# Transposing P per token tile, and gating as if no row were routed, with two rows replaced in DRAM

## The chip, the core and the metric

One core of a Trainium2 chip. The metric is device time in microseconds of one execution, the median of the runs; the profile is of one execution. The engines are called by the profile's names: PE is TensorE, DVE VectorE, ACT ScalarE, POOL GpSimd, SP the engine that issues most DMAs; SPq and ACTq are the issuing queues of SP and ACT.

## What is computed

Token matrix x of 2048 x 640, in bfloat16. It is normalized row by row; an attention over the last 512 keys of each of 32 heads (head size 192) and a small routed MLP both start from it, and the second gates the first:

```python
xn = _layernorm(x, axis=-1)
s = _A_ref(xn, A_k_cache, A_v_cache, A_wq, A_wo)      # softmax(q k') v, then wo
g = _silu(_B_ref(xn, B_w_r, B_w_gate, B_w_up, B_w_down))
return x + s * g
```

In `_B_ref`, r = xn @ w_r picks the C = 2 rows with the largest scores; only these two go through the MLP, and their result is added to their rows of xn:

```python
g = _silu(x_sel @ w_gate)
u = x_sel @ w_up
y = (g * u) @ w_down
r_sel = _sigmoid(jnp.take_along_axis(r, idx, axis=1))
y = y * r_sel.reshape(B, C, 1)
return x + upd.reshape(B, S, D)     # upd: zero but for the two rows of y
```

So for 2046 of the 2048 rows the gate is silu(xn) alone.

## The kernel before

**The loop.** Heads go in 8 groups of 4 (two pairs each); tokens in 4 tiles of 512. A step is (group, token tile, pair), 64 steps, each of two blocks: block b (0 to 127) handles 256 tokens as two tiles of 128 (a = 0, 1) against one pair of heads. Blocks 0 to 11 and 126 to 127 are written out by hand (`FIRST`, `LAST`); blocks 12 to 125 follow one list, `BLOCK`, whose tokens are emitted in this order:

- A, B: the two halves of q's products for the next step (L340); after B, ACT copies q out of PSUM (L352). The pool for q has one pair of banks, so the next A waits for that copy.
- S0, S1: scores of the two token tiles (L367), two PSUM buffers; M0, M1: their row maxima on DVE (L372); E0, E1: exponentials on ACT (L377) into `p_ring`, which holds two blocks.
- P: `o_item(b - 2)`: P times V (L406) for both token tiles, division by the row sum (reciprocal L413; scaled copies L417 on DVE, L420 on ACT), and the transpose of the result, oT, by a DMA that SP issues (L423). Between the two tiles' products `bg[b]` is emitted.
- W: `w_item(b - 6)`: the products with wo (L447), added to the fp32 accumulator `s_acc` on DVE (L470).
- m: what stands in `mid[b]`; l, the end of the block: `end[b]`, then `loads[b]`.

Every engine executes its own instructions in the order in which they were emitted, SP and the other DMA queues too. The row sums come for free: V has a further column of ones (L175), so that the products of P with V carry the sum in column 192.

**P's transpose.** `exps` issues a DMA transpose of P on SP: for blocks in `SPLIT` one per token tile, 128 x 1024, right behind that tile's exponentials (L381); for the others one of both tiles, 128 x 2048, behind E1 (L383). `pT_ring` holds three blocks. P's exponentials of block b may not overwrite `p_ring` before block b - 2 has been read by its transpose.

**The routed rows.** In dictionaries by block (`bg`, `mid`, `end`, `loads`) the kernel plans the MLP beside the loop. `m_r` (blocks 12 to 27) makes the scores; `m_round`, `m_rows`, `m_top`, `m_sel`, `m_tok`, `m_own` find the two rows (the scores are turned by a TensorE transpose, L690) and fetch their x by an indirect DMA on POOL; `m_gather` normalizes the two rows on DVE (blocks 34 to 40, L774 at the end); `m_xsT` turns them; `m_ffn` makes gate and up products (L787) at blocks 42, 49 and 57, with h on DVE (L797, L798), turned by SP (L801); `m_down` the down products (L826) at 62 and 69, and `m_sum` (block 70) adds four partial sums on POOL (L839 to L842). Then y is written to DRAM and read back to all 128 partitions (L844, L846). Weights of the MLP are loaded by ACT's queue in blocks 33 to 66.

**The gate.** For each of 16 tiles n of 128 tokens, `m_add(n)` at block 71 + 2n halves xn on POOL (L850) and adds each of the two rows of y, times a column that is 0.5 in the routed row and 0 elsewhere (L853, L854): five POOL operations of 128 x 640. `m_gate(n)` takes tanh on ACT at block 75 + 2n (L860) and multiplies on DVE in the middle of block 76 + 2n (L863), in place in xn. From block 107 on, `fin_load` fetches x again (L912), `fin_pre` multiplies `s_acc` by the gate and adds x on POOL (L917, L918), and in the last head group `w_item` multiplies the last products by the gate (L473), adds (L475, L478) and stores.

Of the kernel before, what the change touches and what calls it, by code (L numbers as in the profile page):

```python
# [21 lines left out]
def kernel(ctx, tc, A_x, A_k_cache, A_v_cache, A_wq, A_wo, B_x, B_w_r, B_w_gate, B_w_up, B_w_down, out):  # L22
    nc = tc.nc
    P = 128
# [147 lines left out]
    eps_t = const.tile([P, 1], FP32, name="eps_t")  # L172
    nc.vector.memset(eps_t, EPS)
    nc.vector.tensor_copy(out=ident, in_=ident_f)
    nc.gpsimd.memset(v_ring[:, :, :, Dh:Dh + 1], 1.0)  # L175

    mv = const.tile([P, NTB, 2], FP32, name="mv")
    rstd = const.tile([P, NTB], FP32, name="rstd")
# [108 lines left out]
    NS = len(steps)  # L287
    NB = 2 * NS
    HEAD = 12
    SPLIT = (0, 1, 2, 3, NB - 4, NB - 3, NB - 2)  # L290
    qT_of = {}
    fin_x = {}
    fin_pool = {}
# [355 lines left out]
    def m_open():  # L649
        late.close()  # L650
        M["stack"] = ExitStack()
        M["w"] = M["stack"].enter_context(tc.tile_pool(name="moe_w", bufs=1))
        M["s"] = M["stack"].enter_context(tc.tile_pool(name="moe_s", bufs=1))
        M["wr"] = M["s"].tile([P, D], BF16, name="wr_bc", tag="t3")
        nc.gpsimd.dma_start(out=M["wr"], in_=B_w_r.partition_broadcast(P))
        M["r"] = M["s"].tile([P, NTB], FP32, name="r_pn")
        M["xsT"] = M["s"].tile([P, DC, 32], BF16, name="xsT")
        M["xsel"] = M["s"].tile([32, D], BF16, name="xsel")
        nc.gpsimd.memset(M["xsel"], 0.0)
        M["pick"] = M["s"].tile([P, 2], FP32, name="pick")  # L660
        nc.gpsimd.memset(M["pick"], 0.0)
        for c in range(4):
            nc.gpsimd.affine_select(out=M["pick"], in_=M["pick"], compare_op=ALU.not_equal, fill=1.0, base=-32 * c,
                                    pattern=[[-1, 2]], channel_multiplier=1)
        M["oh"] = M["s"].tile([P, NTB, 2], FP32, name="oh")
        M["iota"] = M["s"].tile([P, NTB], FP32, name="iota")
        nc.gpsimd.iota(M["iota"], pattern=[[P, NTB]], base=0, channel_multiplier=1, allow_small_or_imprecise_dtypes=True)

    def m_r(n):
        def f():  # L670
# [6 lines left out]

    def m_round():

        M["r_b"] = M["s"].tile([P, NTB], BF16, name="r_b")  # L680
        nc.vector.tensor_copy(out=M["r_b"], in_=M["r"])
        M["base"] = M["s"].tile([NTB, 1], FP32, name="base")
        nc.gpsimd.iota(M["base"], pattern=[[0, 1]], base=0, channel_multiplier=P, allow_small_or_imprecise_dtypes=True)
        M["cpos"] = M["s"].tile([P, NCD], FP32, name="cpos")
        nc.gpsimd.iota(M["cpos"], pattern=[[1, NCD]], base=0, channel_multiplier=0, allow_small_or_imprecise_dtypes=True)

    def m_rows():

        r_ps = f_tile([NTB, P], BF16, "r_ps")
        nc.tensor.transpose(out=r_ps, in_=M["r_b"], identity=ident)  # L690
        M["rows"] = M["s"].tile([NTB, P], FP32, name="r_rows", tag="t2")
        nc.vector.tensor_copy(out=M["rows"], in_=r_ps)

    def m_top():

        top = M["s"].tile([NTB, 8], FP32, name="top8")
        loc = M["s"].tile([NTB, 8], U32, name="loc8")
        nc.vector.max(out=top, in_=M["rows"])
# [33 lines left out]
    def m_own():  # L732
        sel = M["s"].tile([2, 2, 2], FP32, name="sel")
        for q in range(2):
            nc.vector.tensor_tensor(out=sel[:, q, :], in0=M["best"][0:2, q, :], in1=ident_f[0:2, 0:2], op=ALU.mult)
        M["own"] = M["s"].tile([2, 2], FP32, name="own")
        nc.vector.reduce_sum(out=M["own"], in_=sel, axis=AX.X)
        idx_i = M["s"].tile([2, 1], I32, name="idx_i")
# [14 lines left out]

    def m_gather():

        def mask():
            for j in range(2):
                nc.vector.tensor_scalar(out=M["oh"][:, :, j], in0=M["iota"], scalar1=M["best"][:, 1, j:j + 1], scalar2=0.5,
                                        op0=ALU.is_equal, op1=ALU.mult)

        def begin():
            M["mv2"] = M["s"].tile([2, 2], FP32, name="mv2")
            M["rs2"] = M["s"].tile([2, 2], FP32, name="rs2")
            ln_stats(M["xg"], M["mv2"], parts=2)
            M["nw"] = rsqrt_newton(M["mv2"][:, 1:2], M["rs2"][:, 0:1], 2, 1)

        def newton(q):
            for f in M["nw"][3 * q:3 * q + 3]:
                f()

        def apply():
            mv2, rs2 = M["mv2"], M["rs2"]
            ln_nmr(mv2[:, 0:1], rs2[:, 0:1], rs2[:, 1:2])
            nc.vector.tensor_scalar(out=M["xsel"][0:2, :], in0=M["xg"], scalar1=rs2[:, 0:1], scalar2=rs2[:, 1:2], op0=ALU.mult, op1=ALU.add)  # L774
        return [mask, begin] + [lambda q=q: newton(q) for q in range(4)] + [apply]

    def m_xsT():
        nc.sync.dma_start_transpose(out=M["xsT"], in_=M["xsel"])
# [2 lines left out]
    def m_ffn(fb):  # L781
# [12 lines left out]
        def act():  # L794
            th = M["th"]
            M["h"] = M["s"].tile([P, P], BF16, name="h")
            nc.vector.scalar_tensor_tensor(out=th[:, 2], in0=th[:, 2], scalar=1.0, in1=th[:, 0], op0=ALU.add, op1=ALU.mult)  # L797
            nc.vector.scalar_tensor_tensor(out=M["h"], in0=th[:, 2], scalar=0.5, in1=th[:, 1], op0=ALU.mult, op1=ALU.mult)  # L798

        def turn():  # L800
            nc.sync.dma_start_transpose(out=M["hT"][:, fb * 4:(fb + 1) * 4, :].rearrange("p c t -> p (c t)"), in_=M["h"])  # L801
# [10 lines left out]
    def m_sig():  # L812

        sg = M["s"].tile([P, 2], FP32, name="sg")
        nc.scalar.activation(out=sg, in_=M["best"][:, 0, :], func=ACT.Tanh, scale=0.5)
        nc.vector.tensor_scalar(out=sg, in0=sg, scalar1=0.5, scalar2=0.5, op0=ALU.mult, op1=ALU.add)
# [18 lines left out]
    def m_sum():  # L835
# [4 lines left out]
        y_sb = M["s"].tile([2, D], BF16, name="y_sb", tag="t3")  # L840
        nc.gpsimd.tensor_tensor(out=y4[:, 0:2, :], in0=y4[:, 0:2, :], in1=y4[:, 2:4, :], op=ALU.add)
        nc.gpsimd.tensor_tensor(out=y_sb, in0=y4[:, 0, :], in1=y4[:, 1, :], op=ALU.add)  # L842
        y_d = tc.dram_tile([2, D], BF16, name="y_d")
        nc.gpsimd.dma_start(out=y_d, in_=y_sb)  # L844
        M["y_bc"] = M["w"].tile([P, 2, D], BF16, name="y_bc", tag="w")
        nc.gpsimd.dma_start(out=M["y_bc"], in_=y_d.partition_broadcast(P))  # L846

    def m_add(n):
        def f():
            nc.gpsimd.tensor_scalar(out=xn[:, n, :], in0=xn[:, n, :], scalar1=0.5, scalar2=None, op0=ALU.mult)  # L850
            for j in range(2):
                yh = M["s"].tile([P, D], BF16, name="yh", tag="t1")
                nc.gpsimd.tensor_scalar(out=yh, in0=M["y_bc"][:, j, :], scalar1=M["oh"][:, n, j:j + 1], scalar2=None, op0=ALU.mult)  # L853
                nc.gpsimd.tensor_tensor(out=xn[:, n, :], in0=xn[:, n, :], in1=yh, op=ALU.add)  # L854
        return f

    def m_gate(n):
        def a():
            M["tz"] = M["s"].tile([P, D], FP32, name="tz", tag="t2")
            nc.scalar.activation(out=M["tz"], in_=xn[:, n, :], func=ACT.Tanh)  # L860

        def b():
            nc.vector.scalar_tensor_tensor(out=xn[:, n, :], in0=M["tz"], scalar=1.0, in1=xn[:, n, :], op0=ALU.add, op1=ALU.mult)  # L863
        return a, b

    bg[11].append(m_open)

# [3 lines left out]
        spot(b).append(m_r(n))  # L871
    end[24].append(m_r(15))
    mid[28].append(m_round)
    bg[28].append(m_rows)
    for b, it in enumerate((m_top, None, m_sel, m_tok, m_own, *m_gather())):
        if it is not None:
            spot(29 + b).append(it)
    loads[40].append(m_xsT)
# [15 lines left out]
    bg[69].append(m_down(1))  # L894
    bg[70].append(m_sum)
    for n in range(NTB):
        bg[71 + 2 * n].append(m_add(n))
        a, b = m_gate(n)
        bg[75 + 2 * n].append(a)
        mid[76 + 2 * n].append(b)  # L900


    def fin_open():
# [5 lines left out]
    def fin_load(n):  # L909
        def f():  # L910
            fin_x[n] = fin_pool["x"].tile([P, D], BF16, name="x_fin")
            nc.sync.dma_start(out=fin_x[n], in_=x_v[:, n, :])  # L912
        return f

    def fin_pre(n):
# [101 lines left out]
```

## Time and profile before

| | |
|---|---|
| runs, device time | 795.93 us median of 3 (792.62, 795.93, 797.04) |
| profiled execution, device time | 794.4 us |
| its span | 792.6 us |
| PE clock granted | 1.00 |
| SP: oT transposes (L423) | 126, 1209/1235/2445 ns (min/median/max) to issue |
| SP: x again (L912) | 16, 399/799/1311 ns to issue, 160 KB each, 3.5 us to landing |
| DMA queue 1 (SP's) | 130.83 MB, 433568 packets, 94.6% of 16 engines' span |
| HBM | read 39.98 MB, written 2.62 MB |

How to read the profile: a line such as L372 is a line of the kernel. A group's row gives out<-in, count, busy us, mean ns of one, and the idle time of the engine before them with what ended it. In a timeline row the first number is the start in us, the second the length, x the number of merged instructions, and the bracket the idle time before the first with what released it. For a DMA the row of SPq is the issue alone; landing is later. In the view of one tile, three numbers after the count are shortest, median and longest in ns. In the waits, the three numbers are us in total, times, and the longest.

### The profile page before, as it was taken

To read this page: it belongs to the slowest core of one execution; us is meant where nothing else is said; L and a number is where in the kernel's file an instruction comes from. 1 tells how busy PE (TensorE), PEld (TensorE's weight loads), DVE (VectorE), ACT (ScalarE), POOL (GpSimd) and SP (SyncE) were. 2 spreads that over 40 slices of the span, in tenths; PEclk is the share of its full clock that TensorE was granted. 3 is DMA by queue.
4 is the path that set the end of the run, shared out by engine and by line. 5 is a ranking of instruction groups with operands and counts; after the bars stand their busy time and mean duration, and the time that the engine had idled before them with its cause. 6 is when DMAs were issued, how large, how long until landed. Compare 5 with 4: busy or idle time off the path is not lost.

```text
span 792.6 us, 26635 instructions
## 1 busy us (share of the span) xinstructions
PE 778.2 (98%) x11357; PEld 576.8 (73%) x11357; DVE 594.5 (75%) x1091; ACT 526.1 (66%) x952; POOL 313.8 (40%) x248
## 2 busy tenths in 40 slices
PE   8899999999999999999999999999999999999997
PEld 4457677777777776777777777777777777777775
DVE  7898788877777676767666777777777776766785
ACT  6676666666666766666666667767777776666662
POOL 1334111021110101001001499998996413565865
PEclk9999999999999999999999999999999999999999
DMA  9989999799999999999999999989999899999993
GB/s 233 196 175 168 164 188 165 149 191 164 180 205 173 184 221 195 183 178 216 182 206 167 180 190 183 155 158 184 158 191 164 148 190 179 197 185 168 180 173 87
DMA packets 443319, 141.77 MB, mean 179 GB/s; under 512 B 410436, under 2 KB 442696, under 8 KB 443200
## 3 DMA queue, kind: packets, MB, share of 16 engines
q1 hardware_dynamic: 433568, 130.83, 94.6%
q10 hardware_dynamic: 8672, 6.72, 3.4%
q0 software_dynamic: 960, 2.52, 1.1%
q8 instruction: 89, 1.46, 0.8%
q14 instruction: 30, 0.25, 0.1%
HBM read 39.98 MB, written 2.62 MB: 54 GB/s over the span
## 4 chain that ended last, share of the span: by engine, by line
PE 89%; DMA 4%; DVE 3%; ACT 2%; issue 1%; SPq 0%; ACTq 0%; DVEq 0%
PE w L447 25%; PE q_ps L340 23%; PE o_ps L406 20%; PE s L367 19%; DMA pT<-pexp 4%; ACT pexp L377 1%; PE q_ps L309 1%; DVE nm L372 1%; DMA v_sb<-in_A_v_cache_dram 1%; ACT xnT L283 0%; DMA x_in<-in_A_x_dram 0%; PE tp L282 0%; PE gu_ps L787 0%; DVE fin_t L473 0%; DVE fin_o L475 0%
## 5 line engine op out<-in xcount | busy, mean ns | idle before, releaser
L372 DVE TENSOR_REDUCE nm<-s 128x2 f32<-128x1024 f32 x256 | 313.0, 1223 | 123.1 <-PE s L367 117.2
L377 ACT ACTIVATE pexp<-s,nm 128x512 bf16<-128x512 f32 x512 | 324.3, 689 | 110.5 <-DVE nm L372 67.7
L340 PE MATMUL q_ps<-xnT,wq_g 64*128 64x512 bf16 (+1 forms) x2340 | 232.8, 323 | 1.1 <-ACT qT L352 1.0
L447 PE MATMUL w<-wo_g,oT 64*128 64x320 bf16 x3072 | 231.1, 296 | 0.4 <-ACT o_sb L420 0.2
L367 PE MATMUL s<-kT,qT 64*128 64x512 bf16 x1536 | 211.8, 376 | 1.7 <-ACT pexp L377 1.4
L447 PEld LDWEIGHTS <-oT 64*128 64x128 bf16 x3072 | 171.5, 94 | 57.2 <-issue 1.2
L406 PEld LDWEIGHTS <-pT 64*128 64x128 bf16 x4096 | 177.6, 94 | 31.2 <-issue 2.8
L406 PE MATMUL o_ps<-v_sb,pT 64*128 64x193 bf16 x4096 | 195.6, 243 | 3.0 <-DMA pT<-pexp 1.6
L420 ACT ACTIVATE o_sb<-o_ps,rl 128x192 bf16<-128x192 f32 x250 | 91.7, 418 | 126.8 <-DVE rl L413 120.4
L340 PEld LDWEIGHTS <-wq_g 64*128 64x128 bf16 x2340 | 127.2, 99 | 46.4 <-issue 1.9
L151 POOL COPY wo_g<-wo_g 64x1920 bf16<-64x1920 bf16 x32 | 57.7, 1807 | 213.5 <-DMA wo_g<-in_A_wo_dram 178.1
L367 PEld LDWEIGHTS <-qT 64*128 64x128 bf16 x1536 | 85.6, 94 | 55.9 <-issue 2.4
L470 DVE TENSOR_TENSOR s_acc<-s_acc,w 128x320 f32<-128x320 f32 x192 | 85.0, 484 | 32.8 <-PE w L447 32.7
L352 ACT ACTIVATE qT<-q_ps 128x1024 bf16<-128x1024 f32 x114 | 92.5, 811 | 4.8 <-PE q_ps L340 0.2
L417 DVE TENSOR_TENSOR o_sb<-o_ps,rl 128x384 bf16<-128x384 f32 x131 | 73.0, 558 | 4.5
L121 POOL COPY k_perm<-k_raw 128x768 bf16<-128x768 bf16 x30 | 25.1, 851 | 123.9 <-DMA k_raw<-in_A_k_cache_dram 92.7
L853 POOL TENSOR_SCALAR yh<-y_bc,oh 128x640 bf16<-128x640 bf16 x32 | 61.2, 1912 | 4.9 <-DMA y_bc<-y_d 3.3
L854 POOL TENSOR_TENSOR xn<-xn,yh 128x640 bf16<-128x640 bf16 x32 | 45.7, 1429 | 2.7
L413 DVE RECIPROCAL rl<-o_ps 128x2 f32<-128x2 f32 x256 | 30.6, 160 | 12.9 <-PE o_ps L406 7.6
L918 POOL TENSOR_TENSOR s_acc<-s_acc,x_fin 128x640 f32<-128x640 f32 x16 | 22.4, 1399 | 31.5 <-DMA x_fin<-in_A_x_dram 31.1
L850 POOL TENSOR_SCALAR xn<-xn 128x640 bf16<-128x640 bf16 x16 | 30.0, 1873 | 0.8
L478 POOL TENSOR_TENSOR fin_o<-fin_t,s_acc 128x640 bf16<-128x640 f32 x12 | 18.5, 1542 | 17.4 <-DVE fin_t L473 11.0
(132 smaller groups left out, 261.5 us busy)
## 6 DMA issues: line engine op xcount, KB each, us to landing
wo_g<-in_A_wo_dram SPq DMA_DIRECT2D x32, 240.0 KB, 4.2
k_raw<-in_A_k_cache_dram SPq DMA_DIRECT2D x32, 192.0 KB, 3.3
v_sb<-in_A_v_cache_dram SPq DMA_DIRECT2D x32, 192.0 KB, 4.1
wq_g<-in_A_wq_dram SPq DMA_DIRECT2D x14, 288.0 KB, 3.6
wq_g<-in_A_wq_dram SPq DMA_DIRECT2D x14, 192.0 KB, 3.7
x_fin<-in_A_x_dram SPq DMA_DIRECT2D x16, 160.0 KB, 3.5
pT<-pexp SPq DMA_TRANSPOSE x134, 4.8
oT<-o_sb SPq DMA_TRANSPOSE x126, 3.6
```

The lines of the kernel that those rows point to most:

```text
L151: nc.gpsimd.tensor_copy(out=grp[g][("wo", pr)][half(1), cs, :], in_=grp[g][("wo", pr)][half(0), cs, :])
L340: mm = nc.tensor.matmul(q_ps[k][:, 0:n] if type(q_ps) is list else q_ps[:, k, 0:n], lhsT=wq[half(r), dc, c:2 * Dh:3], rhs=xnT[half(r), tok ...
L352: nc.scalar.activation(out=out, in_=q_ps[:, :, 0:n], func=ACT.Copy, scale=scale)
L367: nc.tensor.matmul(s_of[b, a][:, r, :], lhsT=qT_of[i][half(r), c, u * P:(u + 1) * P], rhs=grp[g][("kT", pr)][half(r), :, c, :], start=(c = ...
L372: rm = nc.vector.tensor_reduce(out=nm_of[b, a], in_=s_of[b, a], axis=AX.X, op=ALU.max, negate=True)
L377: nc.scalar.activation(out=p_ring[:, b % 2, a, :, hh, :].rearrange("p (x j) e -> p x j e", x=2), in_=s_of[b, a][:, hh, :].rearrange("p (j ...
L406: nc.tensor.matmul(o_of[b][r][:, a, 0:Dh + 1], lhsT=pT_ring[half(r), b % RP, a, k, :], rhs=v_ring[half(r), (g * PAIRS + pr) % RV, k, 0:Dh ...
L417: nc.vector.tensor_tensor(out=o_sb, in0=src, in1=rl[:, r].unsqueeze(2).unsqueeze(3).to_broadcast([P, 2, 3, HK]), op=ALU.mult)
L420: nc.scalar.activation(out=o_sb[:, a], in_=src[:, a], func=ACT.Copy, scale=rl[:, r, a:a + 1])
L447: nc.tensor.matmul(w_ps[r][:, 0:HD], lhsT=oT_ring[half(r), bs[pr] % RT, c, :], rhs=grp[g][("wo", pr)][half(r), c, cs], start=(pr == 0 and ...
L470: nc.vector.tensor_tensor(out=acc, in0=acc, in1=src, op=ALU.add)
L853: nc.gpsimd.tensor_scalar(out=yh, in0=M["y_bc"][:, j, :], scalar1=M["oh"][:, n, j:j + 1], scalar2=None, op0=ALU.mult)
```

## The change

Two things at once.

**P in halves.** `SPLIT` now holds 0 to 3 and all blocks from 12 to 126: one DMA transpose of 128 x 1024 per token tile.

**The gate without the routed rows.** The ones in V become twos, so that the row sums, and with them everything divided by them, change by a factor of 2 that takes up the 0.5 of silu: silu(z) = 0.5 z (1 + tanh(z/2)). The gate of tile n is made at block 71 + 2n from xn as it is: tanh(x/2) on ACT, then two POOL operations, tz * x and + x. In the block after it SP stores the tile to a DRAM tensor `gate_d`. The two routed rows' gates are made apart at block 103 (`m_own_gate`) from the two rows' xn + y, and scattered by an indirect DMA over their rows of `gate_d`. From block 107 on SP loads the gates back into xn, tile by tile, beside x. With that the steps that spread y over all tokens go: the mask, y to DRAM and back, `m_add`, and the gate's product on DVE.

Beside this: the scores are turned by a DMA transpose of 128 x 128 on SP in block 28 in place of PE's, and the search for maxima moves from the end of block 29 to the middle of block 30; `m_tok` and `m_own` are joined in block 33; the last step of the two rows' normalization moves from DVE to ACT; h is made by three POOL operations in place of two on DVE.

```diff
-    nc.gpsimd.memset(v_ring[:, :, :, Dh:Dh + 1], 1.0)
+    nc.gpsimd.memset(v_ring[:, :, :, Dh:Dh + 1], 2.0)
...
-    SPLIT = (0, 1, 2, 3, NB - 4, NB - 3, NB - 2)
+    SPLIT = (0, 1, 2, 3, *range(HEAD, NB - 1))
...
     def m_rows():
-
-        r_ps = f_tile([NTB, P], BF16, "r_ps")
-        nc.tensor.transpose(out=r_ps, in_=M["r_b"], identity=ident)
-        M["rows"] = M["s"].tile([NTB, P], FP32, name="r_rows", tag="t2")
-        nc.vector.tensor_copy(out=M["rows"], in_=r_ps)
+        M["rT"] = M["s"].tile([P, P], BF16, name="r_rowsT")
+        nc.sync.dma_start_transpose(out=M["rT"], in_=M["r_b"])
...
-            nc.vector.tensor_scalar(out=M["xsel"][0:2, :], in0=M["xg"], scalar1=rs2[:, 0:1], scalar2=rs2[:, 1:2], op0=ALU.mult, op1=ALU.add)
-        return [mask, begin] + [lambda q=q: newton(q) for q in range(4)] + [apply]
+            nc.scalar.activation(out=M["xsel"][0:2, :], in_=M["xg"], func=ACT.Identity, bias=rs2[:, 1:2], scale=rs2[:, 0:1])
+        return [begin] + [lambda q=q: newton(q) for q in range(4)] + [apply]
...
-            nc.vector.scalar_tensor_tensor(out=th[:, 2], in0=th[:, 2], scalar=1.0, in1=th[:, 0], op0=ALU.add, op1=ALU.mult)
-            nc.vector.scalar_tensor_tensor(out=M["h"], in0=th[:, 2], scalar=0.5, in1=th[:, 1], op0=ALU.mult, op1=ALU.mult)
+            nc.gpsimd.tensor_tensor(out=th[:, 2], in0=th[:, 2], in1=th[:, 0], op=ALU.mult)
+            nc.gpsimd.tensor_tensor(out=th[:, 2], in0=th[:, 2], in1=th[:, 0], op=ALU.add)
+            nc.gpsimd.tensor_tensor(out=M["h"], in0=th[:, 2], in1=th[:, 1], op=ALU.mult)
...
-        y_d = tc.dram_tile([2, D], BF16, name="y_d")
-        nc.gpsimd.dma_start(out=y_d, in_=y_sb)
-        M["y_bc"] = M["w"].tile([P, 2, D], BF16, name="y_bc", tag="w")
-        nc.gpsimd.dma_start(out=M["y_bc"], in_=y_d.partition_broadcast(P))
-
-    def m_add(n):
+        nc.gpsimd.tensor_tensor(out=M["xsel"][0:2, :], in0=M["xsel"][0:2, :], in1=y_sb, op=ALU.add)
+        M["y4"], M["y_sb"] = y4, y_sb
...
+    def gate_of(tz, x, y):
+        nc.scalar.activation(out=tz, in_=x, func=ACT.Tanh, scale=0.5)
+        nc.gpsimd.tensor_tensor(out=tz, in0=tz, in1=x, op=ALU.mult)
+        nc.gpsimd.tensor_tensor(out=y, in0=tz, in1=x, op=ALU.add)
+
+    def m_gate(n):
         def f():
...
+            tz = M["s"].tile([P, D], FP32, name="tz", tag="t2")
+            gate_of(tz, xn[:, n, :], xn[:, n, :])
         return f
...
+    def m_away(n):
+        return lambda: nc.sync.dma_start(out=gate_v[:, n, :], in_=xn[:, n, :])
+
+    def m_own_gate():
+        gate_of(M["y4"][:, 3, :], M["xsel"][0:2, :], M["y_sb"])
+        nc.gpsimd.indirect_dma_start(out=gate_d, out_offset=bass.IndirectOffsetOnAxis(ap=M["idx"][:, 0:1], axis=0),
+                                     in_=M["y_sb"], in_offset=None, bounds_check=S - 1)
...
     for n in range(NTB):
-        bg[71 + 2 * n].append(m_add(n))
-        a, b = m_gate(n)
-        bg[75 + 2 * n].append(a)
-        mid[76 + 2 * n].append(b)
+        bg[71 + 2 * n].append(m_gate(n))
+        loads[72 + 2 * n].append(m_away(n))
+    bg[103].append(m_own_gate)
...
             nc.sync.dma_start(out=fin_x[n], in_=x_v[:, n, :])
+            nc.sync.dma_start(out=xn[:, n, :], in_=gate_v[:, n, :])
```

More of the change, by code (lines that the diff above doesn't have):

```diff
@@ L664, in m_open @@
                                     pattern=[[-1, 2]], channel_multiplier=1)
-        M["oh"] = M["s"].tile([P, NTB, 2], FP32, name="oh")
-        M["iota"] = M["s"].tile([P, NTB], FP32, name="iota")
-        nc.gpsimd.iota(M["iota"], pattern=[[P, NTB]], base=0, channel_multiplier=1, allow_small_or_imprecise_dtypes=True)
+        M["r_b"] = M["s"].tile([P, P], BF16, name="r_b")
+        nc.gpsimd.memset(M["r_b"], 0.0)
     def m_r(n):
@@ L678, in m_round @@
     def m_round():
-        M["r_b"] = M["s"].tile([P, NTB], BF16, name="r_b")
-        nc.vector.tensor_copy(out=M["r_b"], in_=M["r"])
+        nc.vector.tensor_copy(out=M["r_b"][:, 0:NTB], in_=M["r"])
         M["base"] = M["s"].tile([NTB, 1], FP32, name="base")
@@ L697, in m_top @@
         loc = M["s"].tile([NTB, 8], U32, name="loc8")
+        M["rows"] = M["s"].tile([NTB, P], FP32, name="r_rows", tag="t2")
+        nc.vector.tensor_copy(out=M["rows"], in_=M["rT"][0:NTB])
         nc.vector.max(out=top, in_=M["rows"])
@@ L737, in m_own @@
         nc.vector.reduce_sum(out=M["own"], in_=sel, axis=AX.X)
-        idx_i = M["s"].tile([2, 1], I32, name="idx_i")
+        M["idx"] = idx_i = M["s"].tile([2, 1], I32, name="idx_i")
         nc.vector.tensor_copy(out=idx_i, in_=M["own"][:, 1:2])
@@ L754, in m_gather @@
     def m_gather():
[L756 to L759, printed above, removed]
         def begin():
@@ L815, in m_sig @@
         nc.scalar.activation(out=sg, in_=M["best"][:, 0, :], func=ACT.Tanh, scale=0.5)
-        nc.vector.tensor_scalar(out=sg, in0=sg, scalar1=0.5, scalar2=0.5, op0=ALU.mult, op1=ALU.add)
+        nc.vector.tensor_scalar(out=sg, in0=sg, scalar1=0.25, scalar2=0.25, op0=ALU.mult, op1=ALU.add)
         nc.vector.tensor_tensor(out=M["pick"], in0=M["pick"], in1=sg, op=ALU.mult)
@@ L842, in m_sum, with m_tok_own @@
         nc.gpsimd.tensor_tensor(out=y_sb, in0=y4[:, 0, :], in1=y4[:, 1, :], op=ALU.add)
-        y_d = tc.dram_tile([2, D], BF16, name="y_d")
-        nc.gpsimd.dma_start(out=y_d, in_=y_sb)
-        M["y_bc"] = M["w"].tile([P, 2, D], BF16, name="y_bc", tag="w")
-        nc.gpsimd.dma_start(out=M["y_bc"], in_=y_d.partition_broadcast(P))
-    def m_add(n):
-        def f():
[L850 to L854, printed above, removed]
-        return f
[L857 to L864, printed above, removed]
+        nc.gpsimd.tensor_tensor(out=M["xsel"][0:2, :], in0=M["xsel"][0:2, :], in1=y_sb, op=ALU.add)
+        M["y4"], M["y_sb"] = y4, y_sb
+    gate_d = tc.dram_tile([S, D], BF16, name="gate_d")
+    gate_v = gate_d.rearrange("(n p) d -> p n d", p=P)
+    def gate_of(tz, x, y):
[3 more added lines that the diff above has]
+    def m_gate(n):
+        def f():
+            tz = M["s"].tile([P, D], FP32, name="tz", tag="t2")
+            gate_of(tz, xn[:, n, :], xn[:, n, :])
+        return f
+    def m_away(n):
[4 more added lines that the diff above has]
+                                     in_=M["y_sb"], in_offset=None, bounds_check=S - 1)
+    def m_tok_own():
+        m_tok()
+        m_own()
     bg[11].append(m_open)
@@ L873 @@
     mid[28].append(m_round)
-    bg[28].append(m_rows)
-    for b, it in enumerate((m_top, None, m_sel, m_tok, m_own, *m_gather())):
+    loads[28].append(m_rows)
+    for b, it in enumerate((None, m_top, None, m_sel, m_tok_own, None, *m_gather())):
         if it is not None:
```

## The prediction

> **What bounds the kernel now.** I read the page first: span, busy times, chain.
>
> ```profile
> span 792.6 us, 26635 instructions
> PE 778.2 (98%) x11357; PEld 576.8 (73%) x11357; DVE 594.5 (75%) x1091; ACT 526.1 (66%) x952; POOL 313.8 (40%) x248
> ...
> PE 89%; DMA 4%; DVE 3%; ACT 2%; issue 1%; SPq 0%; ACTq 0%; DVEq 0%
> ```
>
> TensorE is busy 98% of the span and makes up 89% of the chain. As its busy time is modelled, I tested it by the period. The timeline gives the start of each row maximum (L372); two blocks, one step of the loop, lie between these two:
>
> ```profile
> 541.06 1.22 DVE L372 TENSOR_REDUCE nm<-s 128x2 f32<-128x1024 f32 x1 [0.96 <-PE s L367]
> ...
> 552.84 1.23 DVE L372 TENSOR_REDUCE nm<-s 128x2 f32<-128x1024 f32 x1 [0.97 <-PE s L367]
> ```
>
> That is 11.78 us. Of the 56 such steps from block 12 (86.7 us) to block 124 (753.5 us), 40 take 11.78 within 0.015, with whatever else lies in them: this is TensorE's own work at a granted clock of 1.00, and the change takes nothing out of it. 56 x 11.78 = 659.7, measured 666.8: all that is lost over these blocks is **7.1 us**. I went through the steps that are longer:
> - routed-row products (L787, L826), steps of blocks 42, 48, 56, 62, 68: 0.70 + 0.70 + 0.70 + 0.67 + 0.67 = 3.4 us, work that stays (step 48 is 1.84 too long, and 0.70 is taken from step 42, which has nothing else);
> - step 28, with the transpose of the scores (L690): 0.44;
> - late transposed P, steps 40, 48, 60 (0.43, 1.14, 0.50) and crumbs in 24, 44, 58: about 2.5;
> - steps 82, 84 and 98, where a gate's product on VectorE (L863) stands ahead of a row maximum: 0.8.
>
> The late P is seen in the waits and in block 48:
>
> ```profile
> ACT pexp L377 <- DMA pT<-pexp: 28.9, 25, 2.5
> ```
>
> ```profile
> 300.55 1.22 DVE L372 TENSOR_REDUCE nm<-s 128x2 f32<-128x1024 f32 x1 [0.96 <-PE s L367]
> ...
> 303.35 1.27 ACT L377 ACTIVATE pexp<-s,nm 128x512 bf16<-128x512 f32 x2 [2.50 <-DMA pT<-pexp]
> ...
> 304.50 1.02 ACT L352 ACTIVATE qT<-q_ps 128x1024 bf16<-128x1024 f32 x1
> ...
> 305.58 0.73 PE L340 MATMUL q_ps<-xnT,wq_g 64*128 64x256 bf16 x10 [0.45 <-ACT qT L352]
> ```
>
> The exponentials write a ring of two blocks, so those of block b wait until the transpose of block b-2 has read its P. Here the row maximum ends at 301.77, but ACT starts at 303.35; the copy of q behind it ends at 305.52, and TensorE, which has one pair of banks for q, starts 0.45 us late. Mostly such a wait costs nothing: 28.9 us of waits, some 2.5 us of them paid.
>
> **The change, part by part.**
>
> *P in halves.* One transpose of 128x2048 per block becomes two of 128x1024, the first behind the first exponentials. The kernel has both forms:
>
> ```profile
> L383 SPq DMA_TRANSPOSE pT<-pexp x120: 1333/2490/4674, 42.0 to 754.7; - x120
> L381 SPq DMA_TRANSPOSE pT<-pexp x14: 1244/1277/2116, 19.4 to 769.3; - x14
> ```
>
> In blocks 12 to 125 the SP rows of the timeline add up to 4.97 us per block: pT 2.53, oT 1.34, the rest 1.10, in a block of 5.89. At its least a half costs SP as much as a whole (1.24 and 1.33), so the issue is per instruction; the rest of the whole's 2.5 us is waiting for room, since the page shows DMA 90% busy or more in most slices. Two unhindered halves make 2 x 1.28 + 1.34 + 1.10 = 5.0 us; if all the waiting stayed it would be 4.97 + 1.25 = 6.2. I take the first: between 19.4 and 30.9 us six halves, with weight loads and an oT between them, took 1.24 to 1.30 us each and landed within 4.8. The first half now starts where block 541.06's first exponentials end, 2.6 us into its block, where the whole started 6.9 us in. With a landing of 4.3 to 4.8 us it is over 5 us ahead of the exponentials two blocks later (2 x 5.89 + 1.3 us in); the second half has the whole's start and half its size. So the late P goes: **-2.0 us** of the 2.5, bounds -2.5 and 0 (SP and the queue are fullest in blocks 41 to 66, where weights come in on ACT's queue as well, and this is where the waits are).
>
> The Trainium skill (DMA: Bandwidth & Descriptors, section "Rules for kernel authors") speaks against this edit: coalesce small transfers into one large one, as under 64 KB one pays mostly overhead. Here a half is still 256 KB, and by landing (4.3 to 4.8 us for halves, 4.8 median for wholes) the overhead is indeed most of it. What it would do is the first rival below.
>
> *Routing.* The scores' transpose leaves TensorE (L690) and goes to SP as one DMA transpose, 1.2 us as other small ones: **-0.44 us**. The maxima move from the end of block 29 to the middle of 30; about 1.3 us of VectorE ahead of the second row maximum, which has 0.9 us of room there and ACT's o_sb behind it: 0. The rest of the chain keeps its blocks.
>
> *The two rows' normalization* goes from VectorE to ACT, in the middle of block 40:
>
> ```profile
> 253.39 1.26 ACT L377 ACTIVATE pexp<-s,nm 128x512 bf16<-128x512 f32 x2 [0.96 <-DVE nm L372]
> ...
> 254.48 0.14 DVE L197 SCALAR_TENSOR_TENSOR rs<-mv,rs 2x1 f32<-2x1 f32 x1
> 254.66 0.43 DVE L774 TENSOR_SCALAR xsel<-xg,rs 2x640 bf16<-2x640 bf16 x1
> 254.77 1.02 ACT L352 ACTIVATE qT<-q_ps 128x1024 bf16<-128x1024 f32 x1
> ...
> 256.54 0.72 PE L340 MATMUL q_ps<-xnT,wq_g 64*128 64x256 bf16 x10
> ```
>
> This is an added wait. In ACT's order it stands ahead of the first exponentials, and its bias comes from L197, which stands behind the additions of W. So ACT starts it at 254.65, ends at 255.55 (0.92 as L191, the same form over 128 rows), exponentials to 256.85, q's copy to 257.9, and TensorE starts at about 258.1, not 256.54: **+1.5 us**, bounds 0 (if slack behind makes it up) and 2.2 (ACT's whole delay, 255.6 - 253.4).
>
> *h on GpSimd*, three operations: rows of this size lie between 0.23 (L238, 4 columns) and 1.40 us (L917, 640 columns); even 4.2 us ends before SP reaches the transpose at the end of the block: 0.
>
> *Gates.* Gone are on GpSimd L850 30.0, L853 61.2 and L854 45.7 us, and L863 16.1 us on VectorE. New are 32 GpSimd operations of 1.40 (L917) to 1.54 us (L478), 45 to 49 us; tanh stays on ACT. GpSimd is off the path, so its 90 us are worth nothing; VectorE's 16 take with them the 0.8 us of steps 82, 84 and 98: **-0.7 us**, bounds -0.8 and 0. The first tanh moves from block 75 to 71 and takes yp's buffer: yp has been read at 438.6 us, it starts about 443.5. Sixteen stores of 160 KB from SP: each waits for its gate, with the next halves of P behind it, but the gate is done some 0.6 us into the block at whose end SP gets there, 5 us of cover; beyond that, P still has 5 us. Sixteen loads of 160 KB beside x (L912, 0.78 us each): SP then has 2 x 1.28 + 1.25 + 2 x 0.5 to 0.8 + the weights, 5.4 to 6.3 us in blocks 109 to 114 and about 5 behind: half a microsecond of backlog, within the slack. The scatter in block 103 ends in about 12 us (a store 3.1, tanh 0.75, two operations of 1.5, indirect 1.0 + 4.4), and SP wants it four blocks, 23.6 us, later: 0.
>
> Sum: -2.0 - 0.44 + 1.5 - 0.7 = **-1.6 us**, bounds -3.7 and +1.8. The profiled execution took 794.4 us around its span of 792.6, so 792.8 by it; the median of the runs is 795.93, 1.5 above, and on that scale the forecast is **794.3 us**. 0.5%, 4.0 us, is about what a measurement of this kernel can tell from no change; the three runs alone spread over 4.4.
>
> **The rivals.**
> - *SP becomes the bound* (slower). SP issues in order. It decides if a half costs on average over (5.89 - 1.34 - 1.10) / 2 = 1.73 us. For: at 752 to 772 us halves that follow on each other take 2.0 to 2.1, and the six there average 1.7. Against: there three come in a row, and blocks are 4.9 us. At 1.85 a block grows by 0.25 us, 114 blocks by 28: 824 us; with all the waiting kept, 6.2, by 0.33 x 114: 833. The rule quoted above points here.
> - *The wait on ACT is all that is left*: halves come no earlier in blocks 41 to 66, since SP is full there (5.7 of 5.9 us in many). -0.44 + 1.5 - 0.7 is about 0: 796.3.
> - *More is won than counted*: over 4 us. Without the products that stay 3.7 us are lost from block 12 on, and the blocks before 12 and after 124 keep their order; it needs a shorter period. 791. Against: forty equal steps.
>
> **How the numbers follow.** Forecast 0.62, ACT's wait alone 0.19, SP 0.12, more won 0.07. Faster by over 0.5%: 0.09; within: 0.77; slower: 0.14 (SP, and a little of the second). The range takes in the bounds, 792.2 to 797.7, and the runs' spread of about 2 to each side: 790.5 to 800.
>
> **What would show it.** Period still 11.78; waits of pexp for pT near 0; L381 about 230 times at 1.3 to 1.6 us; step 28 at 11.78; step 40 some 1.5 too long with TensorE waiting for qT; GpSimd some 90 us less busy; steps 82 and 98 at 11.78. I am wrong if the period grows evenly from block 12 on (SP), or in blocks 71 to 123 alone (the gates' traffic).

## The result, and the profile after

| | median, us | lowest to highest | runs |
|---|---|---|---|
| before | 795.97 | 792.62 to 798.0 | 20 |
| after | 800.89 | 797.02 to 804.65 | 20 |

The ratio is 1.0057, 95% interval 1.0045 to 1.007: slower by about 4.5 us (4.9 between the two medians). The forecast was 794.3 us with "within 0.5%" as the likeliest case; the time lies above the range's upper end of 800.

The profiled execution took 801.89 us, with a span of 800.1 us. The page's span, busy times and chain:

```profile
span 800.1 us, 26957 instructions
...
PE 779.0 (97%) x11356; PEld 573.6 (72%) x11356; DVE 578.7 (72%) x1066; ACT 527.2 (66%) x954; POOL 229.5 (29%) x211
...
PE 82%; DMA 6%; DVE 4%; ACT 3%; POOL 2%; issue 2%; SPq 1%; ACTq 0%; DVEq 0%; POOLq 0%
```

TensorE has the same work (779.0 against 778.2 us) in a span that is 7.5 us longer. GpSimd lost 84 us of work, VectorE 16. What is new in the chain is DMA: 4% became 6%. The view of pT and the waits show that P in halves does what it was to do:

```profile
L381 SPq DMA_TRANSPOSE pT<-pexp x238: 1231/1262/3087, 19.6 to 776.6; - x119
L383 SPq DMA_TRANSPOSE pT<-pexp x8: 1762/2390/3223, 42.9 to 88.3; - x8
```

```profile
ACT pexp L377 <- DMA pT<-pexp: 4.5, 2, 2.7
...
PE w L447 <- DMA oT<-o_sb: 3.6, 4, 2.0
...
PE o_ps L406 <- DMA pT<-pexp: 3.0, 5, 1.1
```

The exponentials waited 28.9 us for pT before, now 4.5. But TensorE itself now waits for transposes: W's products for oT 3.6 us, P times V for pT 3.0 (before: nothing and 1.6).

Where in time? I took the start of the first row maximum (L372) of every second block from the timeline and summed what each two-block step takes over 11.775 us, the length of most steps:

| traced run | start of block 12 | blocks 12 to 108, too long | blocks 108 to 124, too long | behind block 124 |
|---|---|---|---|---|
| before | 86.7 | 7.32 | 0.10 | 39.1 |
| after | 87.6 | 7.04 | **6.34** | 39.7 |

Of 7.5 us, 6.2 came in blocks 108 to 124, above all the steps of 112, 114 and 122 (1.72, 2.22, 1.25). That is the stretch in which `fin_load` reads the gates back. Block 113 in the timeline, and ahead of it the oT transpose before with the copy that completes its o_sb:

```profile
681.85 0.73 ACT L420 ACTIVATE o_sb<-o_ps,rl 128x192 bf16<-128x192 f32 x2 [1.29 <-DVE rl L413]
...
689.70 1.25 SPq L423 DMA_TRANSPOSE oT<-o_sb  x1
...
692.35 0.63 SPq L146 DMA_DIRECT2D wo_g<-in_A_wo_dram  x1
...
693.07 0.54 SPq L912 DMA_DIRECT2D x_fin<-in_A_x_dram  x1
693.66 0.43 SPq L913 DMA_DIRECT2D xn<-gate_d  x1
694.20 1.35 SPq L381 DMA_TRANSPOSE pT<-pexp  x1
...
694.25 0.84 PE L406 MATMUL o_ps<-v_sb,pT 64*128 64x193 bf16 x16 [1.12 <-DMA pT<-pexp]
...
695.65 1.96 SPq L423 DMA_TRANSPOSE oT<-o_sb  x1
...
699.68 0.99 PE L447 MATMUL w<-wo_g,oT 64*128 64x320 bf16 x12 [2.04 <-DMA oT<-o_sb]
```

The queue goes on without a pause: each issue starts 0.05 to 0.11 us behind the end of the one before it. W's products for a block want an oT that SP turned only at 695.65 and that landed 4 us later; TensorE stood for 2.04 us. SP was late: the o_sb of the transpose at 689.70 had been complete since 682.58, 7.1 us earlier, more than a block. (There is one transpose per block, in order; the next copies end at 689.42 and 696.07, so the transpose at 695.65 is that of the first of them.) The same stretch before the change, SP's queue, and likewise an o_sb and its transpose:

```profile
681.19 0.73 ACT L420 ACTIVATE o_sb<-o_ps,rl 128x192 bf16<-128x192 f32 x2 [0.97 <-DVE rl L413]
...
684.41 1.80 SPq L423 DMA_TRANSPOSE oT<-o_sb  x1
...
689.38 0.55 SPq L912 DMA_DIRECT2D x_fin<-in_A_x_dram  x1
690.03 1.25 SPq L423 DMA_TRANSPOSE oT<-o_sb  x1
691.38 3.20 SPq L383 DMA_TRANSPOSE pT<-pexp  x1
694.63 0.59 SPq L136 DMA_DIRECT2D v_sb<-in_A_v_cache_dram  x1
695.31 0.57 SPq L912 DMA_DIRECT2D x_fin<-in_A_x_dram  x1
695.99 1.23 SPq L423 DMA_TRANSPOSE oT<-o_sb  x1
697.33 2.90 SPq L383 DMA_TRANSPOSE pT<-pexp  x1
```

It was without a pause already: from 664.2 to 700.2 us no gap is longer than 0.2 us, and blocks 109 to 115 hold 5.4 to 5.6 us of issuing each, in blocks of 5.88. The mean over all blocks, 4.97, hides it. But SP was at most 2.5 us late there (the transpose at 684.41), and on time again from 712 us on.

### The profile page after: what moved, and what is told of

Same layout as the page of the kernel before. It is cut to its first block, busy times and chain, and to the rows that moved or that the text cites. A ratio compares the mean times of both kernels' runs of the same rounds, so it can differ in the third digit from the quotient of the medians.

```text
span 800.1 us, 26957 instructions
## 1 busy us (share of the span) xinstructions
PE 779.0 (97%) x11356; PEld 573.6 (72%) x11356; DVE 578.7 (72%) x1066; ACT 527.2 (66%) x954; POOL 229.5 (29%) x211
## 3 DMA queue, kind: packets, MB, share of 16 engines
q1 hardware_dynamic: 441920, 136.12, 100.6%
q8 instruction: 89, 1.46, 0.8%
## 4 chain that ended last, share of the span: by engine, by line
PE 82%; DMA 6%; DVE 4%; ACT 3%; POOL 2%; issue 2%; SPq 1%; ACTq 0%; DVEq 0%; POOLq 0%
PE w L447 22%; PE q_ps L340 22%; PE o_ps L406 19%; PE s L367 18%; DMA pT<-pexp 2%; ACT pexp L377 2%; DMA oT<-o_sb 2%; DVE nm L372 2%; PE q_ps L309 1%; POOL fin_o L478 1%; DMA x_in<-in_A_x_dram 1%; DMA v_sb<-in_A_v_cache_dram 1%; ACT o_sb L420 0%; ACT qT L352 0%; POOL s_acc L918 0%
## 5 line engine op out<-in xcount | busy, mean ns | idle before, releaser
L372 DVE TENSOR_REDUCE nm<-s 128x2 f32<-128x1024 f32 x256 | 313.0, 1223 | 141.0 <-PE s L367 135.5
L420 ACT ACTIVATE o_sb<-o_ps,rl 128x192 bf16<-128x192 f32 x250 | 91.4, 417 | 135.6 <-DVE rl L413 130.5
L151 POOL COPY wo_g<-wo_g 64x1920 bf16<-64x1920 bf16 x32 | 57.3, 1795 | 181.3 <-DMA wo_g<-in_A_wo_dram 180.5
L417 DVE TENSOR_TENSOR o_sb<-o_ps,rl 128x384 bf16<-128x384 f32 x131 | 73.0, 558 | 4.8 <-DVE rl L413 0.4
L846 POOL TENSOR_TENSOR tz<-tz,xn 128x640 f32<-128x640 f32 x16 | 22.4, 1398 | 99.2 <-ACT tz L845 99.2
L918 POOL TENSOR_TENSOR s_acc<-s_acc,xn 128x640 f32<-128x640 f32 x16 | 22.4, 1400 | 42.6 <-DMA xn<-gate_d 37.7
L847 POOL TENSOR_TENSOR xn<-tz,xn 128x640 bf16<-128x640 f32 x16 | 22.4, 1397 | 1.3
L473 DVE TENSOR_TENSOR fin_t<-w,xn 128x320 f32<-128x320 f32 x32 | 14.4, 486 | 10.3 <-PE w L447 9.5
```

Of the source, the lines that this page charges most:

```text
L151: nc.gpsimd.tensor_copy(out=grp[g][("wo", pr)][half(1), cs, :], in_=grp[g][("wo", pr)][half(0), cs, :])
L372: rm = nc.vector.tensor_reduce(out=nm_of[b, a], in_=s_of[b, a], axis=AX.X, op=ALU.max, negate=True)
L417: nc.vector.tensor_tensor(out=o_sb, in0=src, in1=rl[:, r].unsqueeze(2).unsqueeze(3).to_broadcast([P, 2, 3, HK]), op=ALU.mult)
L420: nc.scalar.activation(out=o_sb[:, a], in_=src[:, a], func=ACT.Copy, scale=rl[:, r, a:a + 1])
```

## The experiments

The theories: **S**, SP's queue has no room for the 16 loads behind block 107; **T**, it is the bytes of the gates; **H**, the halves by themselves; **A**, the wait on ACT in block 40; in the last four runs **G**, the gates' path through DRAM (stores, scatter, reading back what was just written), and **R**, room before block 107. Ratios are to the kernel before on the same chip, with 95% intervals; the median of before was 795.25, 795.04 and 795.33 us in the three groups of four.

### One part of the change at a time

**Gates alone** (P in whole):

```diff
-    SPLIT = (0, 1, 2, 3, *range(HEAD, NB - 1))
+    SPLIT = (0, 1, 2, 3, NB - 4, NB - 3, NB - 2)
```

> The gate's part of the change alone; P is transposed whole again as before. Theory S (SP's issue queue is full from block 108 on, because three transposes, two tile loads and the weights take as long to issue as a block lasts): with two transposes a block SP has room again, steps 112 to 122 are at most 0.5 us over 11.78 in all, 795 to 797 us beside 796 of before (the wait for the rows' normalization on ACT stays, about +0.7). Theory T (the gates' 5.2 MB and the halves fill the DMA engines): the gates' bytes are still there, about 798. Theory H (halves are the cost by themselves, wherever they are): 795 to 796.

798.76 us, ratio 1.0037 (1.0019 to 1.0054). Blocks 108 to 124 are 4.37 us too long in its trace (110, 112, 114: 1.16, 0.98, 2.23). Most of the loss is there without any half.

**Halves alone** is the kernel before with the change's `SPLIT`.

> P in halves alone, everything else as before. Theory S: one tile load per block from 108 on, SP needs about 5.2 of 5.9 us, so no pile-up: steps 112 to 122 at 11.78, some of the 2.5 us of late P won, 793.5 to 796. Theory T: half of the loss, about 798. Theory H: the whole loss, 800 or more.

795.19 us, ratio 1.0005 (0.9993 to 1.0017): H falls. The forecast gain appears and is lost again: step 48 goes from 1.85 to 0.77 us too long and step 60 from 0.50 to nothing, but steps 84, 88, 94, 96, 102 and 104 become 0.2 to 0.8 us too long: in just these the gate's product on VectorE (L863) takes 1.44 to 2.02 us in place of 0.82, as it meets GpSimd's work (last section; step 84 was 0.10 too long before already). Over blocks 12 to 108 both traces, this one and that of before, lose 7.32 us.

**Halves up to block 106 only**, with the gates:

```diff
-    SPLIT = (0, 1, 2, 3, *range(HEAD, NB - 1))
+    SPLIT = (0, 1, 2, 3, *range(HEAD, 107), NB - 4, NB - 3, NB - 2)
```

> The changed kernel with P in halves from block 12 to 106 only and whole from 107 to 123, where the gates are loaded. Theory S: no pile-up, 795 to 797. Theory T: fewer transposes at the place of the loads but the same bytes, 799 to 801. Theory H: 95 of 112 blocks still have halves, so about 85% of the loss, 800.

800.58 us, ratio 1.0079 (1.005 to 1.0109): taking the second half from SP in the late blocks relieves nothing that these six runs show (796.31 to 805.25). The trace, 3.17 us too long in blocks 108 to 124, is of the fastest of them. A whole holds SP about as long as two halves: 1.9 to 3.2 us in blocks 109 to 114 of the kernel before.

**Gate loads on GpSimd's queue**, the rest as changed:

```diff
-            nc.sync.dma_start(out=xn[:, n, :], in_=gate_v[:, n, :])
+            nc.gpsimd.dma_start(out=xn[:, n, :], in_=gate_v[:, n, :])
```

> The changed kernel, with the 16 loads of the gate issued by GpSimd's queue in place of SP's; the same bytes at the same places. Theory S: SP is rid of about 0.5 us per block from 108 on, steps 112 to 122 lose under 1 us in all in place of 6.3, 795 to 797. Theory T: the bytes are the same, 800 to 801 as the changed kernel. Theory H: 800 to 801.

799.4 us, ratio 1.0052 (1.0028 to 1.0075). Blocks 108 to 124 fall to 1.8 us, but the kernel is no faster: in its trace step 40 alone is 4.08 us too long. That step holds the move to ACT, so the next four kernels take it back. S had 795 to 797 for each of the three kernels with gates and missed all three; T came within 1 us of them, but had about 798 for halves alone.

### The loads, without the wait on ACT

**Normalization back on VectorE**:

```diff
-            nc.scalar.activation(out=M["xsel"][0:2, :], in_=M["xg"], func=ACT.Identity, bias=rs2[:, 1:2], scale=rs2[:, 0:1])
+            nc.vector.tensor_scalar(out=M["xsel"][0:2, :], in0=M["xg"], scalar1=rs2[:, 0:1], scalar2=rs2[:, 1:2], op0=ALU.mult, op1=ALU.add)
```

> The changed kernel with the rows' normalization back on VectorE. Theory A (the wait on ACT in block 40 carries most of the loss, as in some executions TensorE idles 2 us there and its clock then drops to half for 3.4 us): 796.5 to 798, step 40 at 12.0 to 12.3 in place of 12.95 to 15.9. Theory S (SP's issue room from block 108 on) and theory T (the bytes of the gates from block 108 on): 1 us less than the changed kernel's 800.9, so 799.5 to 800.5, steps 112 to 122 as long as there.

798.13 us, ratio 1.0051 (1.0031 to 1.007), next to 1.0057 with ACT: A isn't most of the loss. The difference, 0.06%, is uncertain by 0.23%, so some 2 us of A can't be ruled out, and the median lies between what A (796.5 to 798) and S and T (799.5 to 800.5) had. In the trace, which is of the fastest of the twelve runs (794.35), step 40 is still 0.74 us too long and blocks 108 to 124 are 2.31.

**Gate loads of 4 of 640 columns** (as the last, and):

```diff
-            nc.sync.dma_start(out=xn[:, n, :], in_=gate_v[:, n, :])
+            nc.sync.dma_start(out=xn[:, n, 0:4], in_=gate_v[:, n, 0:4])
```

> As apply_dve, and each of SP's 16 loads of the gate brings 4 of 640 columns (the two routed rows keep the unrouted gate in the other columns). As many issues on SP, 1/160 of the bytes. Theory S: as apply_dve within 1 us. Theory T: 2 to 4 us less than apply_dve, steps 112 to 122 lose under 1 us in all.

796.73 us, ratio 1.0020 (1.0001 to 1.0038); blocks 108 to 124 are 2.97 us too long in its trace.

**Gate loads on GpSimd's queue** (the edit above, with VectorE's normalization):

> As apply_dve, and the 16 loads of the gate go out from GpSimd's queue: the same bytes, no issue on SP. Theory S: 2 to 4 us less than apply_dve, steps 112 to 122 lose under 2 us. Theory T: as apply_dve within 1 us.

796.5 us, ratio 1.0014 (0.9994 to 1.0034); blocks 108 to 124 are 2.90 us too long in its trace.

**No gate loads**:

> As apply_dve, without the 16 loads (the gate is used as it stands in the buffer, so the two routed rows keep the unrouted gate; stores and scatter stay). Theories S and T: 795 to 796, steps 112 to 122 at 11.78; what is left over 11.78 lies before block 108. Theory A: as apply_dve within 1 us.

794.25 us, ratio 0.9993 (0.9975 to 1.0012): without the 16 loads the loss is gone (0.57 us in blocks 108 to 124 of its trace). From 1.0051, taking the bytes away (1 KB in place of 160 KB, the same 16 issues) wins 0.31%, and taking the issues away as well another 0.27%; moving the issues to another queue, bytes kept, wins 0.37%. By these ratios it is neither S nor T alone, but about half bytes and half issue. That is a best estimate and isn't shown: with four intervals of some 0.2% to each side each of the three differences is uncertain by about 0.27%, and only the whole, 0.58%, is clear. The small loads also bring as many packets as the large ones (441920 on SP's queue in both traces), so "issue" takes those in. Nor do the traces show the split: theirs lose more in blocks 108 to 124 with small loads, or with loads on GpSimd's queue, than the trace with large loads on SP's, which is of a run 3.8 us below its median. The windows over blocks 108 to 116 (stretch and its length; busy us of PE, PEld, DVE, ACT, POOL with counts; granted clock; DMA share; GB/s), first of the kernel before:

```profile
659.23:706.42 47.19, 47.19 (x709) 35.98 (x705) 33.03 (x56) 31.14 (x57) 21.87 (x16) 1.00 1.06 186
```

of the kernel with whole loads on SP's queue and VectorE's normalization:

```profile
656.64:704.94 48.30, 47.28 (x709) 35.19 (x705) 33.03 (x57) 31.29 (x57) 21.05 (x15) 1.00 1.09 200
```

of the kernel with loads of 4 columns:

```profile
659.25:708.58 49.33, 47.46 (x708) 35.04 (x704) 33.03 (x56) 31.30 (x57) 21.75 (x15) 1.00 1.07 177
```

and of the kernel without gate loads:

```profile
656.30:703.98 47.68, 47.28 (x709) 35.23 (x705) 33.03 (x56) 31.25 (x57) 21.43 (x15) 1.00 1.11 184
```

The DMA share is above 1.0 in all four: the transfers fill the engines in this stretch before any gate is loaded. With small loads fewer bytes flow than before (177 against 186 GB/s), and the stretch is 2.14 us longer all the same; with whole loads, in that one trace, it is 1.11 longer.

The result on GpSimd's queue fits a section of the Trainium skill (DMA: Bandwidth & Descriptors, "Issuing engines are not separate DMA queues"): DMAs of all issuing engines interleave on the same 16 DMA engines, and a second issuer saves only issue time. Here, as far as the ratios tell, it took the issue's share of the loss and left the rest. That section of the Trainium skill calls that time "usually small relative to the DMA itself", and so it is here, 0.42 us of issue against 3.3 us to landing (medians of L913, loads on SP's queue); on a queue that was late already it could still count.

### The loads alone, and the loads elsewhere

**Eleven more loads of x in the kernel before**, and the same **with halves**:

```diff
             nc.sync.dma_start(out=fin_x[n], in_=x_v[:, n, :])
+            if n < 11:
+                nc.sync.dma_start(out=fin_pool["o"].tile([P, D], BF16, name="fin_o"), in_=x_v[:, n, :])
```

> The kernel before with eleven more loads of 160 KB on SP's queue, one in each of the blocks 107 to 117, behind the load of x_fin (the same rows of x, into a buffer that nothing reads until the output needs it). No gate is stored or read back, P is transposed in whole. Theory S (the loads fill SP's queue from block 108 on, through their issue time and through the queues of transfers behind them): 797 to 799, ratio 1.0025 to 1.005, with blocks 108 to 124 some 2 to 4 us too long in the trace, as in the kernel with the gates alone (4.37 us, ratio 1.0037). Theory G (the loss comes from the gates' own path: the stores of blocks 72 to 102, the scatter, or reading back what was just written): 795, ratio within 0.0015 of 1, and blocks 108 to 124 below 0.5 us, as before.

798.83 us, ratio 1.0049 (1.003 to 1.0068), blocks 108 to 124 3.51 us too long, steps 112 and 114 1.14 and 2.35: G falls. Eleven loads of 160 KB of x, put on SP there, make nearly the whole loss. SP's queue in blocks 113 and 114 of that kernel:

```profile
691.26 0.42 SPq L914 DMA_DIRECT2D fin_o<-in_A_x_dram  x1
691.79 1.25 SPq L423 DMA_TRANSPOSE oT<-o_sb  x1
693.14 3.48 SPq L383 DMA_TRANSPOSE pT<-pexp  x1
696.68 0.58 SPq L136 DMA_DIRECT2D v_sb<-in_A_v_cache_dram  x1
697.36 0.57 SPq L912 DMA_DIRECT2D x_fin<-in_A_x_dram  x1
697.99 0.41 SPq L914 DMA_DIRECT2D fin_o<-in_A_x_dram  x1
698.50 1.24 SPq L423 DMA_TRANSPOSE oT<-o_sb  x1
```

691.79 to 698.50 is 6.71 us for one round of the queue, in which TensorE needs 5.88. The transfer of P isn't squeezed by the added load (3.48 us, 3.20 before): in this round the load simply comes on top.

> The same eleven loads in the kernel that has only P by halves (ratio 1.0005 without them). Theory S: 798 to 800, ratio 1.003 to 1.006, and more than the loads cost with P in whole if the halves' longer issuing counts (each block issues about 0.3 us more); blocks 108 to 124 3 us or more too long. Theory G: 795.4, ratio within 0.0015 of 1.0005.

799.07 us, ratio 1.005 (1.0031 to 1.007): the loads cost the same with P in halves, so the halves' second issue is not what filled the queue.

**Gates made in every block, read back from block 91 on**, on GpSimd's queue (and the same with SP's):

```diff
-        return lambda: nc.sync.dma_start(out=gate_v[:, n, :], in_=xn[:, n, :])
+        return lambda: nc.gpsimd.dma_start(out=gate_v[:, n, :], in_=xn[:, n, :])
...
+    def m_back(n):
+        return lambda: nc.gpsimd.dma_start(out=xn[:, n, :], in_=gate_v[:, n, :])
...
-        bg[71 + 2 * n].append(m_gate(n))
-        loads[72 + 2 * n].append(m_away(n))
-    bg[103].append(m_own_gate)
+        bg[71 + n].append(m_gate(n))
+        loads[72 + n].append(m_away(n))
+        loads[91 + n].append(m_back(n))
+    bg[89].append(m_own_gate)
...
-            nc.sync.dma_start(out=xn[:, n, :], in_=gate_v[:, n, :])
```

VectorE's normalization stays in both.

> Meant to beat both: xsel applied on DVE as before the change, P by halves, the gates made in every block from 71 on (token tile n in block 71+n), stored and read back on GpSimd's queue (read back in block 91+n), the two rows replaced in block 89. SP then has no gate traffic at all. Theory S: SP is as in the kernel without the loads (794.25, ratio 0.9993), less the stores: 793 to 794.5, ratio 0.997 to 0.9993, and blocks 108 to 124 below 1 us. Theory T (the bytes in the rings of transfers matter, whichever queue issues them): the 5 MB now fall into blocks 72 to 106, where v and wo are loaded, and the waits for oT and pT appear there: 796 to 798. A further risk, which both have: GpSimd's gate work in every block holds up VectorE's operations, each collision about 1 us.

795.08 us, ratio 1.0002 (0.9981 to 1.0022): between what S and T gave, and no gain over the kernel before. Step 114 still is 1.67 us too long, though no gate moves there; steps 44 and 52 lose 1.38 and 1.64, before any gate is made: there the exponentials wait for pT up to 3.5 us, and TensorE 1.19 and 1.47 us for the copy of q behind them. This is late P, in blocks where SP is up to 5.2 us behind.

> The same placing in time, but the gates are stored and read back on SP's queue. Theory S, as the trace of the kernel with its 16 loads has it (SP occupied 5.4 to 5.5 of 5.88 us in the blocks 71 to 106 already): a store or a load in each of the blocks 72 to 106 fills it there, and the loss moves from blocks 108 to 124 to blocks 90 to 108, where W's products wait for oT: 796.5 to 799, ratio 1.002 to 1.005. Theory R (there is room before block 107, only two loads in one block are too many): 793 to 794.5, as on GpSimd's queue.

803.18 us, ratio 1.0085 (1.0058 to 1.0112): S, not R, and worse than S had it (796.5 to 799). Already the steps 78 to 82, with the stores of one gate per block, cost 4.5 us (SP turns an oT in 2.42 us at 504.94, and W's products wait 1.89 us for it), steps 90 and 98 another 2.4, and blocks 108 to 124 lose 3.5 though no gate moves there. The other steps from 72 to 106 stay at 11.78: SP can take one more DMA per block for a while, but falls behind, and is still 4.8 us late in blocks 108 and 109.

## Why the prediction was wrong

**The step that failed: "half a microsecond of backlog, within the slack".** Its sum for one block wasn't far off: in blocks 109 to 111 SP issues for 5.2 to 5.5 us, where it had 5.4 to 6.3. It took the backlog from that sum alone. But in these blocks SP was full and up to 2.5 us late before the change, as its own timeline shows, and what is added there, 0.43 us of issue and 0.1 us between issues for each load, finds little room: the lateness grows from block to block, and other issues grow with it (a kT transpose 2.59 us at 684.57, an oT 1.77 at 681.34). How late SP was can be read from the traces: the time from the end of the copies that complete an o_sb (L417, L420) to the issue of its transpose (L423).

| traced run | SP late in blocks 71 to 106, mean, us | most in blocks 107 to 124, us | blocks 108 to 124, too long, us |
|---|---|---|---|
| before | 0.1 | 2.5 | 0.1 |
| no gate loads | 1.4 | 3.5 | 0.6 |
| eleven loads of x in the kernel before | 0.1 | 3.9 | 3.5 |
| whole loads on SP, VectorE's normalization | 1.4 | 5.1 | 2.3 |
| loads of 4 columns | 1.2 | 5.8 | 3.0 |
| after | 1.5 | **7.1** | 6.3 |

So in place of half a microsecond it was 7.1 us, and the slack didn't cover that. With P in whole (the loads of x in the kernel before) SP was less late, 3.9 us, when TensorE lost time; there it is also pT that comes late (TensorE waits 1.15 us for it at 706.46). The 16 loads were sized at 0 and measured 0.58% by the kernel without them, some 4.6 us (3.9 between the medians). The prediction's own sign for it, a loss "in blocks 71 to 123 alone (the gates' traffic)", is what the trace shows, but for blocks 108 to 124 alone.

The other steps:

- *Late P, -2.0*: the waits went as said (28.9 to 4.5 us), steps 48 and 60 with them, 1.6 us. Step 40 was late P too, as counted: in the kernel before, block 39's transpose, issued at 253.25, landed 7.2 us later, and block 41's exponentials began then, at 260.52. With halves alone this wait is gone, yet the step is 0.51 us too long, by a collision on VectorE (last section). By itself the edit brings nothing that can be measured (1.0005), since VectorE's gate products lose in other steps. And late P comes back where SP is late: step 52 is 0.82 us too long after the change, with 2.7 us of waiting for pT.
- *The scores' transpose, -0.44*: step 28 is at 11.78, but step 30, with the maxima that were to cost 0, is 0.17 us too long.
- *Normalization on ACT, +1.5*: step 40 went from 0.44 to 1.17 us too long in three traces, so +0.7, or +1.2 if its late P is taken as won above, by the mechanism foreseen (in the fourth trace, with the loads on GpSimd's queue, it is 4.08: last section); this is block 40 after the change:

```profile
255.17 0.14 DVE L197 SCALAR_TENSOR_TENSOR rs<-mv,rs 2x1 f32<-2x1 f32 x1
...
255.40 0.92 ACT L766 ACTIVATE xsel<-xg,rs 2x640 bf16<-2x640 bf16 x1 [2.27 <-issue]
...
256.22 1.23 ACT L377 ACTIVATE pexp<-s,nm 128x512 bf16<-128x512 f32 x2
...
258.41 0.62 PE L340 MATMUL q_ps<-xnT,wq_g 64*128 64x256 bf16 x8 [1.00 <-ACT qT L352]
```

- *The gate's product off VectorE, -0.7*: step 98 is at 11.78 and step 84 too; step 82 still loses 0.48 in this trace and nothing in the one without loads, where step 98 loses 0.18.
- *The sum of the rest*: the kernel without loads, with VectorE's normalization, is to be 3.1 us faster by the other terms. Its trace, of the second fastest of twelve runs, is 2.5 us shorter over blocks 12 to 108; its median is 0.6 us lower (interval 2.0 lower to 1.0 higher). So by the trace the other terms came to four fifths of their size, by the medians to two thirds at most.
- *Rival "SP becomes the bound"*: right queue, wrong mechanism. It hung on the cost of a half, over 1.73 us on average; halves took 1.46, and up to block 108 most steps stayed at 11.78. Halves of 256 KB cost nothing that can be measured (1.0005); a P in pieces below the 64 KB of the quoted rule isn't tried in any run.

**What stays open.** How the lost time divides between issue and bytes. Why the gate loads on GpSimd's queue were no help with the normalization on ACT (1.0052) and seem to be with it on VectorE (1.0014): the one trace of the first has a slow clock in block 40, told below, but one trace doesn't say how often.

## What to carry to other kernels

Price an added DMA in the stretch where it is issued, and price how late its queue is, not how long it issues per block; a mean over the loop hides seven full blocks. Issues that start 0.1 us behind one another are a warning, not a proof: in the kernel without gate loads SP issues for 5.38 us or more in 30 of the 36 blocks 71 to 106, and the steps 72 to 106 lose 0.16 us in all. What tells is the time from the end of a transfer's source to its issue. What is late is a different transfer behind the added one, here oT or pT. And a DMA moved to another queue buys back its issue at most, not its bytes.

## What the runs showed of the hardware

**An operation of VectorE can wait for a running one of GpSimd.** In block 40 of the kernel with the normalization back on VectorE:

```profile
253.57 1.81 POOL L151 COPY wo_g<-wo_g 64x1920 bf16<-64x1920 bf16 x1 [18.15 <-DMA wo_g<-in_A_wo_dram]
...
253.75 1.80 DVE L766 TENSOR_SCALAR xsel<-xg,rs 2x640 bf16<-2x640 bf16 x1
```

The same operation took 0.43 us before the change (L774). Likewise L197 took 1.28 us in place of 0.14 with halves alone (254.12 to 255.40, L151 running to 255.39). Step 40 is 0.74 and 0.51 us too long in these two kernels; before the change the same two operations took 0.43 and 0.14. In the kernel before, L863 takes over 1.3 us (normally 0.82) in block 82 (507.68, L854 running until 508.53), and in steps 84 and 98, the three that the prediction saw as too long by a gate's product. The Trainium skill (GPSIMD Engine Reference, "8. Key points") says that the two engines share their SBUF interfaces; the traces agree. The price in blocks 40, 82 and 98 is about what is left of GpSimd's operation: VectorE's ends 0.01 to 0.7 us behind it. Step 84 doesn't fit this (L863 from 519.75 to 521.09, L853 on GpSimd until 521.51), and not every pair collides: at 531.63 L863 takes its 0.82 us while L853 runs (530.18 to 532.07).

**A stall of 2 us can cost twice.** With the loads and halves, TensorE stood 2.06 us for an oT, and from 697.9 us its clock was at half for 3.4 us. The windows before and in it (the clock is the third number from the end):

```profile
694.00:697.90 3.90, 1.84 (x26) 1.17 (x24) 1.23 (x1) 1.88 (x4) 3.76 (x3) 1.00 0.91 157
697.90:701.30 3.40, 3.40 (x20) 1.20 (x16) 0.89 (x2) 0.97 (x1) 1.19 (x2) 0.50 1.05 229
```

The same followed a stall of 2.23 us in block 40 with the gate loads on GpSimd's queue and the normalization on ACT (there L197 had met L151 and taken 1.37 us), and did not follow stalls of 2.04 us (after) and 2.28 us (loads on GpSimd's queue, normalization on VectorE). The Trainium skill (TensorE: Matmul & The Clock Gate, "What's actually happening") gives an idle window of about 3.4 us for it, free-running; the 3.4 us at half clock agree, but here idle times of 2.1 and 2.2 us were enough, in two of the four stalls of 2.0 to 2.3 us between blocks 12 and 124 of the kept traces.
